# Drains behind GpSimd's masking selects and 32 more dummy passes ahead of the first transposes, in a windowed attention followed by a two-layer product

## The chip, the cores and the metric

The kernel runs on one core of a Trainium2 chip. The metric is the device time of one execution in microseconds (us): 211.31 us in the median of three runs, 210.72 to 211.42. The core has a matrix engine (TensorE, PE in the profile; its weight loads are listed apart as PEld), VectorE (DVE), ScalarE (ACT), GpSimd (POOL) and SyncE (SP), each with an instruction queue of its own that it works through in order, and 16 engines for transfers (DMA) that all queues share.

## The reference

Four batches of eight heads, 768 positions of width 64. A position sees the first four positions ("sinks") and the 128 positions up to itself. The result goes through two matrix products with a squared relu between them.

```python
scores = scale * np.matmul(q, k.transpose(0, 1, 3, 2))
is_sink = pos[None, :] < int(n_sink)                       # 4
in_window = (rel >= 0) & (rel < int(window))               # 128
scores = np.where(is_sink | in_window, scores, -1000000000.0)
a = np.exp(scores - np.max(scores, axis=-1, keepdims=True))
a = a / (np.sum(a, axis=-1, keepdims=True) + 1e-09)
out = np.matmul(a, v)
...
x = out.transpose(0, 2, 1, 3).reshape(B * S, H * D)        # 3072 x 512
r = np.maximum(x @ w_in, 0.0)                              # 512 x 2048
return (r * r) @ w_out                                     # 2048 x 512
```

## The kernel before

**An order written by hand.** The kernel first collects some 890 operations (`op(...)`), each with a function that issues its instructions, the engines it may run on, and what it must come after. Then `Plan.run` walks through the string `ORDER` and issues them one by one: `57p+26` is operation 57 on TensorE (p), with 26 dummy passes ahead of it; v, a, g and s stand for VectorE, ScalarE, GpSimd and SyncE. So the order in every queue is fixed, and an engine that waits for one operation holds all that stand behind it in its queue.

**Attention.** For each batch `b` the rows of q and k come in, are transposed (by TensorE for batches 0 and 1, by transposing transfers of SyncE for 2 and 3, line 392), and then worked on in three strips `s` of 256 positions. For a strip and a pair of heads `m`, TensorE makes scores of the window in a PSUM tile `ps` (line 554), ScalarE takes their exponential into `expm` (line 574), and the entries outside the window are set to zero in `expm` by a mask operation (`domask`, lines 579 to 591). TensorE then multiplies the masked tile with v into `po` (line 633), together with the sinks' part (line 608), and VectorE divides by the sum (lines 648, 649) into `xn_sb`. That is brought into the layout of the product's left operand (`px` at line 678, or a transposing transfer) for layer 1 (lines 708 and 874) and layer 2 (lines 969 and 1088).

**The mask operations.** For the strips after the first the order gives each mask to VectorE, as one product with a triangle of ones (line 586), or to GpSimd, as two selects by position (`affine_select` in `triangles`, line 198), each over half of the tile's columns, 128 x 512 elements. Sixteen of the mask operations are GpSimd's; the selects that build the constants at the start use the same function or one of their own, but are not called from `domask`.

**GpSimd's queue.** GpSimd issues in the same queue the loads of w_in (line 278), w_out (line 284), v (line 342) and of q and k (line 331), all of which convert from float32 to bfloat16 on the way. In the timeline of GpSimd such a load occupies it for 0.5 to 1.1 us while it is issued; the transfer itself runs on, and its landing is what the reader of the data waits for. Selects and loads thus stand in one line, for instance `26g 116g` ... `107g` ... `27g 28g`: the last load of w_in, two mask operations, then loads of k.

**The dummy passes.** `warm` (line 168) issues as many matmuls of the identity with itself into the tile that the operation behind it is about to overwrite as `ORDER` asks for with `+n`. Nobody reads what they write. The order asks for them three times: 26 ahead of operation 57, the first transposes, 12 ahead of 69 and 1 ahead of 70. They wait for the identity (line 224) alone; the transposes behind them wait for ScalarE's copy of the first loaded rows (line 179).

Of the kernel before, what the change touches and what calls it, by code (L numbers as in the profile page):

```python
# [15 lines left out]
ALU = mybir.AluOpType  # L16

ORDER = """
0v 8s 9s 1v 56a 55a 3g 7a 10s 57p+26 58p 60v 11s 5g 6g 19g 4g 20g 67v 69p+12 21g 68g 59a 12s 13s 70p+1 83p 71a 61v
72a 14s 15s 22g 23g 84p 63p 102p 65v 85a 62a 86a 24g 25g 79g 103p 106a 73v 74v 64p 75p 76p 104a 66v 91p 113p 78v 93a  # L20
87p 77a 115a 89p 88v 105v 80v 90v 95p 92p 94a 26g 116g 81p 107g 96v 114p 82a 97p 119p 27g 28g 29g 30g 31g 32g 33g
108p 98v 117a 99p 109p 100a 118v 120p 111p 122p 101v 157p 121v 112v 123v 110v 163p 124p 169p 164v 126v 16s 125v 166p
# [52 lines left out]
class Plan:  # L75
# [5 lines left out]
    def op(self, kind, engines, run, after=(), takes=(), reads=(), dma=None, follow=(), late=()):  # L81
        o = Op(kind, engines.split(), run, after, takes, reads, dma, follow, late)
        o.group, o.idx = self.group, len(self.ops)
        self.ops.append(o)
        return o
# [21 lines left out]
def kernel(  # L107
# [11 lines left out]
    nc = tc.nc  # L119
# [24 lines left out]
    ident = consts.tile([128, 128], BF16)  # L144
# [17 lines left out]
    P = Plan(sizes)  # L162
    op = P.op

    def tile_of(slot, name, shape, dtype):
        return pools[slot.pool][slot.buf].tile(shape, dtype, name=name, tag=slot.pool)

    def warm(dst, key=None, h=0):


        for _ in range(P.dummies):
            ins = nc.tensor.matmul(dst, lhsT=ident, rhs=ident, start=True, stop=True,
                                   is_transpose=dst.dtype == BF16)
            if key:
                touch(key, "pe", ins, h)
# [10 lines left out]
    def touch(t, e, ins, *banks, alone=False):  # L186

        before = touched.setdefault(t, [])
        for e_, ins_, banks_, alone_ in before:
            apart = (e == "pe") != (e_ == "pe") or e != e_ and alone and alone_  # L190
            if apart and not set(banks) & set(banks_):
                tc.declare_no_dep(ins.ins, ins_.ins, reason="other bank")
        before.append((e, ins, banks, alone))


    def triangles(e_tile, i, n, fill=0.0):

        nc.gpsimd.affine_select(  # L198
            out=e_tile, in_=e_tile, compare_op=ALU.is_ge, fill=fill, base=i - 1,
            pattern=[[0, n], [1 if i else -1, 128]], channel_multiplier=-1 if i else 1,  # L200
        )
# [163 lines left out]
    def attention(b):  # L365
# [13 lines left out]
        def stage(g):  # L379
            P.group = ("prep", b, g)  # L380
            t0, n = groups[g]
# [16 lines left out]
            for m in range(NP // w) if b not in NATURAL else ():  # L398
# [16 lines left out]
                for part in ((1,), (0,)) if not casted else ((1, 0),):  # L415
                    def transpose_rows(e, m=m, bs=bs):

                        pt = bank_t[b, m, g] = tile_of(bs, "pt", [128, 2, 1024], BF16)
                        warm(pt[:, 0, 0:128], ("pt", b, m, g))
                        for j in range(w):  # L420
                            for ti in (1, 0):
                                for t in range(n):
                                    for h in range(2):
                                        r, o = slice(64 * h, 64 * h + 64), 64 * ((j * 2 + ti) * n + t)
                                        touch(("pt", b, m, g), e, nc.tensor.matmul(  # L425
                                            pt[:, h, o:o + 64],
                                            lhsT=qn_t[b, ti][r, t0 // 128 + t, 128 * (w * m + j):128 * (w * m + j) + 128],
                                            rhs=ident[r, r], is_transpose=True,
                                            start=(j == 0 and ti == 1 and t == 0),
                                            stop=(j == w - 1 and ti == 0 and t == n - 1)), h)  # L430

                    def transpose(e, m=m, bs=bs, part=part, casted=casted):
                        if 1 in part:
                            bank_t[b, m, g] = tile_of(bs, "pt", [128, 2, 1024], BF16)
                        pt = bank_t[b, m, g]
                        warm(pt[:, 0, 0:128], ("pt", b, m, g))
                        qs = {} if casted else {ti: qs_t.pop((b, m, ti, g)) for ti in part}
                        for j in range(w):
                            for ti in part:
                                for t in range(n):  # L440

                                    o = 128 * n * ti if w == 2 else 0
                                    h = j if w == 2 else ti
                                    touch(("pt", b, m, g), e, nc.tensor.matmul(
                                        pt[:, h, o + 128 * t:o + 128 * t + 128],
                                        lhsT=qn_t[b, ti][:, t0 // 128 + t, 128 * (m + 2 * j):128 * (m + 2 * j) + 128]
                                        if casted else qs[ti][:, t, 2 * j:2 * j + 2, :], rhs=ident, is_transpose=True,
                                        start=(t == 0 and (w == 1 or ti == 1)),
                                        stop=(t == n - 1 and (w == 1 or ti == 0))), h)
# [61 lines left out]
            def sink_scores(e):  # L511
                ps = bank_t["sink", b, g] = tile_of(bk, "pk", [128, 512], FP32)
                warm(ps[:, 0:128])
                for m in range(NP):
                    nc.tensor.matmul(ps[32 * m:32 * m + 32, 0:last - lo], lhsT=kb[:, 128 * m:128 * m + 32],  # L515
                                     rhs=qkT_sb[:, m, 0, lo // 128:last // 128, :], start=True, stop=True)
# [12 lines left out]
            for s in range(t0 // 256, last // 256):  # L529
# [3 lines left out]
                for m0 in range(2):  # L533
# [37 lines left out]
                    for j, m in enumerate((m0, m0 + 2)):  # L571
                        def expo(e, s=s, m=m, o=o, sl=exs[j]):
                            x = ex_t[b, s, m] = tile_of(sl, "expm", [128, 2, 512], BF16)
                            nc.scalar.activation(out=x[:, :, o:512], in_=bank_t["s", b, s, m][:, :, o:512],  # L574
                                                 func=AF.Exp, scale=scale)
                        ex = op(f"exp {512 - o}", "act", expo, after=[sc[j % len(sc)]],
                                takes=[exs[j]], reads=[banks[j]])

                        def domask(e, s=s, m=m, o=o):
                            x = ex_t[b, s, m]  # L580
                            if s == 0:
                                mk = mask0.rearrange("p h a c -> p h (a c)").to_broadcast([128, 2, 384])
                                nc.vector.tensor_mul(x[:, :, 128:512], x[:, :, 128:512], mk)
                            elif e == "dve":
                                y = x.rearrange("p h (i c) -> p (h i) c", i=2)
                                nc.vector.tensor_mul(y, y, tri.rearrange("p (o a) c -> p o (a c)", o=1).to_broadcast(
                                    [128, 4, 256]))
                            else:
                                y = x.rearrange("p h (i g c) -> p g (h i) c", i=2, g=2)
                                for i in range(2):  # L590
                                    triangles(y[:, i], i, 4)
                        if biased:
                            masked.append(ex)
                            continue
                        masked.append(op(f"mask {512 - o}", "pool dve" if s else "dve",
                                         domask, after=[ex, c_tri if s else late["masks"]]))
# [722 lines left out]
```

## Time and profile before

| | |
|---|---|
| median of three runs | 211.31 us (210.72 to 211.42) |
| the profiled execution's own time | 210.84 us |
| its span, first to last instruction | 209.1 us |
| TensorE's granted clock, mean | 0.994 |
| busy: TensorE, VectorE, ScalarE, GpSimd | 198.0, 170.7, 126.6, 96.2 us |
| GpSimd's 32 selects on `expm` | 24.6 us |
| GpSimd's issuing of loads of v, q and k | 21.5 + 17.6 + 17.7 us |
| software-issued transfers | 69248 packets, 12.59 MB |

Times in all views are us from the span's start unless marked ns. In the timeline a row gives start, duration, engine, line, operation and tiles, how many instructions were merged, and in brackets the idle time of the engine ahead of it with what ended it. In a view by source line the three numbers are the least, median and greatest duration in ns, and a line below gives the time from a load's issue to its landing in us. An engine's name with a q (POOLq) marks what its sequencer does without the engine. The chain of waits is followed back from the last instruction: at each step to what released it, or to the instruction ahead of it on its engine.

### The profile page before, as it was taken

The numbers are of one execution on the slowest core, as the hardware profiler recorded it, in microseconds if no ns is written. First come the engines' busy times: TensorE is split into PE (matmuls) and PEld (weight loads), VectorE is DVE, ScalarE is ACT, GpSimd is POOL, SyncE is SP. The second block draws the span as 40 slices with busy tenths as digits, with TensorE's granted clock in tenths as the row PEclk, the third lists the DMA queues.
The fourth block names the chain that finished last, engine by engine and source line by source line (L and its number), as shares of the span: only waits on it lengthen the run. The fifth ranks groups of instructions, "written<-read, shape, count | busy, mean of one in ns | idle before, by whom it ended". The sixth has DMA issues, their size and how long they took to land.

```text
span 209.1 us, 5720 instructions
## 1 busy us (share of the span) xinstructions
PE 198.0 (95%) x2402; PEld 162.7 (78%) x2407; DVE 170.7 (82%) x311; ACT 126.6 (61%) x168; POOL 96.2 (46%) x133
## 2 busy tenths in 40 slices
PE   5788999999999999999999999999999999999990
PEld 5547997578457765578798899998789999998990
DVE  3388668888599792689999999999999889999671
ACT  4693034568987726897854936889962067594100
POOL 7879774498899976391670089200050000000000
PEclk9999999999999999999999999999999999999997
DMA  5999999999999999999935249960036111200214
GB/s 158 276 186 205 176 194 215 166 156 205 155 156 133 120 117 157 125 156 190 215 93 155 50 34 103 130 192 0 3 74 144 40 67 38 102 0 3 100 54 150
DMA packets 93882, 26.10 MB, mean 125 GB/s; under 512 B 86816, under 2 KB 91552, under 8 KB 93856
## 3 DMA queue, kind: packets, MB, share of 16 engines
q0 software_dynamic: 69248, 12.59, 81.2%
q1 hardware_dynamic: 24280, 12.94, 29.5%
q8 instruction: 19, 0.31, 0.7%
q10 hardware_dynamic: 328, 0.20, 0.3%
q14 instruction: 7, 0.06, 0.1%
HBM read 27.30 MB, written 6.29 MB: 161 GB/s over the span
## 4 chain that ended last, share of the span: by engine, by line
PE 88%; ACT 3%; DMA 2%; DVE 2%; issue 1%; SPq 1%; POOL 0%; ACTq 0%
PE py L1088 28%; PE pm L708 20%; PE pm L874 17%; PE py L969 7%; PE po L633 6%; PE ps L554 5%; DMA qr<-in_q_dram 2%; ACT expm L574 2%; PE po L608 1%; PE px L678 1%; PE pt L425 1%; SPq L316 1%; PE pk L515 1%; ACT r L719 0%; DVE xn_sb L649 0%
## 5 line engine op out<-in xcount | busy, mean ns | idle before, releaser
L574 ACT ACTIVATE expm<-ps 128x1024 bf16<-128x1024 f32 (+1 forms) x48 | 44.3, 953 | 6.0 <-PE ps L554 5.8
L708 PE MATMUL pm<-xT,w_in_sb 128*128 128x256 bf16 (+1 forms) x320 | 44.1, 294 | 0.4 <-ACT r L719 0.4
L198 POOL TENSOR_SCALAR_AFFINE_SELECT expm<-expm 128x512 bf16<-128x512 bf16 x32 | 24.6, 801 | 40.2 <-ACT expm L574 40.1
L708 PEld LDWEIGHTS <-w_in_sb 128*128 128x128 bf16 x320 | 34.5, 114 | 6.9 <-issue 0.6
L1088 PEld LDWEIGHTS <-gT_sb 128*128 128x128 bf16 x336 | 31.1, 98 | 3.7 <-issue 0.2
L1088 PEld LDWEIGHTS <-sg 128*128 128x128 bf16 x240 | 22.4, 98 | 3.3 <-issue 0.6
L719 ACT ACTIVATE r<-pm 128x1024 bf16<-128x1024 f32 x14 | 14.3, 1024 | 17.4 <-PE pm L708 17.3
L874 PE MATMUL pm<-xs,w_in_sb 128*128 128x128 bf16 (+1 forms) x256 | 23.9, 246 | 0.0
L342 POOL DMA_DIRECT2D v<-in_v_dram x24 | 21.5, 903 | 4.6 <-DMA qn<-in_q_dram 3.8
L874 PEld LDWEIGHTS <-w_in_sb 128*128 128x128 bf16 x256 | 22.0, 114 | 0.2
L331 POOL DMA_DIRECT2D qn<-in_q_dram x20 | 17.6, 885 | 9.1 <-DMA w_out_sb<-in_moe_w_out_dram 4.5
L896 ACT ACTIVATE gT_sb<-r 128x1024 bf16<-128x1024 bf16 x19 | 19.5, 1053 | 2.4 <-DVE r L948 2.3
L1088 PE MATMUL py<-wt,gT_sb 128*128 128x256 bf16 x160 | 20.8, 273 | 0.0
L1088 PE MATMUL py<-wt,sg 128*128 128x256 bf16 x160 | 20.6, 273 | 0.0
L1088 PE MATMUL py<-w_out_sb,gT_sb 128*128 128x256 bf16 x144 | 18.5, 273 | 0.0
L331 POOL DMA_DIRECT2D qn<-in_k_dram x20 | 17.7, 890 | 1.6 <-issue 1.2
L649 DVE TENSOR_TENSOR xn_sb<-po,rc 128x512 bf16<-128x512 f32 (+1 forms) x28 | 17.2, 615 | 1.0
L936 ACT ACTIVATE r<-pm 128x1024 bf16<-128x1024 f32 x11 | 11.1, 1023 | 10.2 <-DVE sg L1046 5.8
L721 DVE TENSOR_SCALAR r<-pm 128x1024 bf16<-128x1024 f32 x10 | 12.1, 1228 | 5.7 <-PE pm L708 5.7
L874 PEld LDWEIGHTS <-qkT 128*128 128x128 bf16 x192 | 16.1, 114 | 0.5 <-issue 0.4
L921 DVE TENSOR_TENSOR t<-t,pm 128x512 f32<-128x512 f32 x24 | 15.5, 679 | 1.1 <-ACT t L179 0.5
L948 DVE CUSTOM_DVE_ANT_1 r<-pm,t 128x1024 bf16<-128x1024 f32 x12 | 14.4, 1218 | 1.9 <-PE pm L874 1.4
(95 smaller groups left out, 320.5 us busy)
## 6 DMA issues: line engine op xcount, KB each, us to landing
out_dram<-osb SPq DMA_DIRECT2D x11, 512.0 KB, 4.0
v<-in_v_dram POOLq DMA_DIRECT2D x24, 128.0 KB, 8.2
qn<-in_k_dram POOLq DMA_DIRECT2D x20, 128.0 KB, 9.4
qn<-in_q_dram POOLq DMA_DIRECT2D x20, 128.0 KB, 8.3
w_in_sb<-in_moe_w_in_dram POOLq DMA_DIRECT2D x4, 512.0 KB, 10.7
w_out_sb<-in_moe_w_out_dram POOLq DMA_DIRECT2D x4, 512.0 KB, 10.5
qr<-in_k_dram SPq DMA_DIRECT2D x4, 256.0 KB, 5.1
qr<-in_q_dram SPq DMA_DIRECT2D x4, 256.0 KB, 5.9
```

The costliest lines, as they stand in the source:

```text
L198: nc.gpsimd.affine_select(out=e_tile, in_=e_tile, compare_op=ALU.is_ge, fill=fill, base=i - 1, pattern=[[0, n], [1 if i else -1, 128]], ch ...
L331: nc.gpsimd.dma_start(out=qn_t[b, ti][:, t, :].rearrange("p (h d) -> p h d", d=D), in_=(q, k)[ti][b, :, 128 * t:128 * t + 128, :].rearrang ...
L342: nc.gpsimd.dma_start(out=v_sb[b % 2][:, t, :, 0:D], in_=v[b, :, 128 * t:128 * t + 128, :].rearrange("h p d -> p h d"))
L574: nc.scalar.activation(out=x[:, :, o:512], in_=bank_t["s", b, s, m][:, :, o:512], func=AF.Exp, scale=scale)
L649: touch(("po", b, s, m0), e, nc.vector.tensor_tensor(out=xn_sb[:, 2 * s:2 * s + 2, :].rearrange("p i (j q h d) -> q p j i h d", j=2, q=2, ...
L708: nc.tensor.matmul(pm[:, i, :], lhsT=w_in_sb[:, fb // 4, kb, fb % 4:512:4], rhs=xT[:, c0 // 256:(c0 + cw) // 256, kb, :], start=(kb == 0), ...
L874: touch(tag, e, nc.tensor.matmul(y[:, bk, :, i, :], lhsT=weights(name, f0 + i, a), rhs=rhs[:, a, :], start=fresh and i == 0 and a == 0, st ...
L896: nc.scalar.activation(out=d, in_=x, func=AF.Square)
L921: touch(tag, e, nc.vector.tensor_tensor(out=T["t"], in0=T["t"], in1=bank(bk), op=ALU.subtract), bk)
L948: touch(tag, e, nc.vector._custom_dve(TENSOR_ADD_SAT, out=r, in0=both(), in1=t, s0=3.4028235e38, s1=0.0), 0, 1)
L969: touch((b, u), e, nc.tensor.matmul(pm[:, i, :], lhsT=gT_sb[:, t, fb, :], rhs=w_out_sb[:, fb, :], start=(fb == 0), stop=(fb == NFB - 1)), i)
L1088: ins = nc.tensor.matmul(y_, lhsT=x[:, i, :], rhs=r_, start=(first or tail and n == 2) and i == 0, stop=i == HB - 1, skip_group_check=not ...
```

## The change

Two edits. `domask` issues a drain of GpSimd behind each of the two selects of a mask operation on GpSimd, 32 in all; a drain is an instruction in GpSimd's queue at which the queue stops until what is ahead of it is over. And the order asks for 58 dummy passes ahead of operation 57 instead of 26, while `warm` makes only the first 18 of a call full passes (128 rows, 128 columns) and those behind them passes of 32 rows and 32 columns. The calls with 12 and 1 passes stay as they were.

```diff
-0v 8s 9s 1v 56a 55a 3g 7a 10s 57p+26 58p 60v 11s 5g 6g 19g 4g 20g 67v 69p+12 21g 68g 59a 12s 13s 70p+1 83p 71a 61v
+0v 8s 9s 1v 56a 55a 3g 7a 10s 57p+58 58p 60v 11s 5g 6g 19g 4g 20g 67v 69p+12 21g 68g 59a 12s 13s 70p+1 83p 71a 61v
...
-        for _ in range(P.dummies):
-            ins = nc.tensor.matmul(dst, lhsT=ident, rhs=ident, start=True, stop=True,
+        for i in range(P.dummies):
+            m, n = (128, 128) if i < 18 else (32, 32)
+            ins = nc.tensor.matmul(dst[0:m, 0:n], lhsT=ident[0:m, 0:m], rhs=ident[0:m, 0:n], start=True, stop=True,
                                    is_transpose=dst.dtype == BF16)
...
                                 y = x.rearrange("p h (i g c) -> p g (h i) c", i=2, g=2)
                                 for i in range(2):
                                     triangles(y[:, i], i, 4)
+                                    nc.gpsimd.drain()
```

## The prediction

> **What bounds the kernel now.** I read the page first: busy shares, the chain of waits, the costliest groups.
>
> ```profile
> span 209.1 us, 5720 instructions
> ...
> PE 198.0 (95%) x2402; PEld 162.7 (78%) x2407; DVE 170.7 (82%) x311; ACT 126.6 (61%) x168; POOL 96.2 (46%) x133
> ...
> PE 88%; ACT 3%; DMA 2%; DVE 2%; issue 1%; SPq 1%; POOL 0%; ACTq 0%
> ```
>
> TensorE sets the time. It runs a fixed order in its queue, so what holds one matmul holds all behind it, and there is almost nothing later to win it back. GpSimd (POOL) is off the chain today, at 46% busy. Its 16 mask operations, of two selects each at line 198 on expm, get 32 drains. GpSimd is also the engine that issues the loads of weights, q, k and v, in one queue with the selects. So the question is what a drain waits for.
>
> **The drain's price.** No row shows a drain between two selects. The nearest are GpSimd's own drains at start and end: a view by source line, the timeline of GpSimd, and the landing of its last load.
>
> ```profile
> L1300 POOLq DRAIN  x1: 193/193/193, 0.4 to 0.4; - x1
> ...
> 0.41 0.11 POOL L1300 MEMSET const-uint8-127<- 128x1 uint8 x1
> ...
> L1314 POOLq DRAIN  x3: 45/93/4215, 152.6 to 208.9; - x3
> ...
> 152.58 2.96 POOL L198 TENSOR_SCALAR_AFFINE_SELECT expm<-expm 128x512 bf16<-128x512 bf16 x4 [20.35 <-ACT expm L574]
> ...
> L342 POOL DMA_DIRECT2D v<-in_v_dram x1: 903/903/903, 127.9 to 127.9; - x1
> ...
> DMA to landing us min/median/max: 6.4/6.4/6.4
> ```
>
> The drain at the start, with no load issued yet, ended at 0.38 + 0.19 = 0.57, some 0.05 us behind the last memset (0.41 + 0.11). The first at the end starts at 152.6 and takes 4.215, to 156.8, though the last select was over at 152.58 + 2.96 = 155.54: 1.2 us more, with all of GpSimd's loads issued since the first drain, the last of them landed at 127.9 + 6.4 = 134.3. The two after that, with nothing in between, took 45 to 93 ns. A drain of GpSimd thus seems to settle something besides the selects, and the loads are what differs. The lower end is 0.05 to 0.1 us per drain; the upper is that it waits until every load issued ahead of it has landed. I take the upper end, because the long row stands apart from the short ones in just this respect; a wait on loads in flight is my inference and is not shown.
>
> In the Trainium skill, "PSUM — Partial Sum Buffer", section "Engine vs sequencer instructions", a drain waits until the engine is fully idle; read as the selects alone that is the lower end and some 212 us, read with the transfers the upper. The long row at the end fits the second reading better.
>
> **First place, 15 us.** GpSimd's and TensorE's timelines, these selects by tile, and landings: of two single loads (min, median and max are one there), and last of all 40 loads of line 331.
>
> ```profile
> 15.28 2.39 POOL L198 TENSOR_SCALAR_AFFINE_SELECT expm<-expm 128x512 bf16<-128x512 bf16 x4 [1.19 <-ACT expm L574]
> ...
> L198 POOL TENSOR_SCALAR_AFFINE_SELECT expm<-expm x4: 628/628/628, 15.3 to 17.0; 128x512 bf16<-128x512 bf16 x4
> ...
> 17.74 1.25 PE L633 MATMUL po<-v,expm 128*128 128x65 bf16 x32
> ...
> L278 POOL DMA_DIRECT2D w_in_sb<-in_moe_w_in_dram x1: 803/803/803, 13.3 to 13.3; - x1
> ...
> DMA to landing us min/median/max: 11.6/11.6/11.6
> ...
> L331 POOL DMA_DIRECT2D qn<-in_k_dram x1: 904/904/904, 17.6 to 17.6; - x1
> ...
> DMA to landing us min/median/max: 8.2/8.2/8.2
> ...
> DMA to landing us min/median/max: 3.5/8.3/14.5
> ```
>
> The last load ahead of the selects is issued at 13.3 and lands 11.6 later, at 24.9. The drain behind the first select holds GpSimd until about 25.0. The other three selects (0.63 each) with their short drains (0.1) end near 27.2; before, at 15.28 + 2.39 = 17.67. TensorE needs the last two for the third quarter of its 32 value matmuls, half-way through that row, near 18.3. It resumes near 27.2: **+8.9**. Queued behind on GpSimd are the next loads, issued at 27.2 instead of 17.6. The first landed at 17.6 + 8.2 = 25.8 behind a backlog; with an empty queue I give it the shortest, 3.5, so 30.7: 4.9 late. That is less than TensorE's 8.9, which covers it; a cover of 4 us is left.
>
> **Second place, 65 to 75 us.**
>
> ```profile
> 64.34 0.88 POOL L331 DMA_DIRECT2D qn<-in_q_dram  x1
> 65.22 1.70 POOL L198 TENSOR_SCALAR_AFFINE_SELECT expm<-expm 128x512 bf16<-128x512 bf16 x2
> 66.88 0.89 POOL L331 DMA_DIRECT2D qn<-in_q_dram  x1
> 67.78 1.35 POOL L198 TENSOR_SCALAR_AFFINE_SELECT expm<-expm 128x512 bf16<-128x512 bf16 x2
> 69.09 1.78 POOL L342 DMA_DIRECT2D v<-in_v_dram  x2
> 70.85 0.89 POOL L331 DMA_DIRECT2D qn<-in_k_dram  x1
> 71.73 2.87 POOL L198 TENSOR_SCALAR_AFFINE_SELECT expm<-expm 128x512 bf16<-128x512 bf16 x4
> ...
> L331 POOL DMA_DIRECT2D qn<-in_q_dram x1: 883/883/883, 64.3 to 64.3; - x1
> ...
> DMA to landing us min/median/max: 14.5/14.5/14.5
> ...
> 70.06 0.92 PE L633 MATMUL po<-v,expm 128*128 128x65 bf16 x16
> ...
> 74.17 1.36 PE L633 MATMUL po<-v,expm 128*128 128x65 bf16 x32
> ...
> 59.23 18.27 SPq L392 DMA_TRANSPOSE qkT<-qn  x9
> ...
> 65.00:76.00 11.00, 10.87 (x193) 8.67 (x192) 9.23 (x18) 6.25 (x10) 10.99 (x15) 1.00 1.97 136
> ```
>
> The stretch's row (busy us of PE, PEld, DVE, ACT, POOL) has GpSimd busy 10.99 of 11.00: here it has no idle time to give. The load of 64.34 landed at 78.8; 4.9 later it is 83.7. The first drain holds the second select until 83.8, over at 84.6. TensorE's values of 70.06 need it; with 8.9 they would come at 79.0, so **+5.6**, total 14.5. Then each batch of loads is followed by a drain that waits for it on an almost empty queue, 3.5 from issue. A load is issued at 84.7 and landed at 88.2; second select to 88.9; three loads, the last issued at 90.8 and landed near 94.3; three selects and drains more to 96.6. The values of 74.17 need the last pair, and would come at 88.7 with 14.5: **+7.9**, total 22.4.
>
> **Later places.** The remaining selects are off the path:
>
> ```profile
> 93.15 1.72 POOL L198 TENSOR_SCALAR_AFFINE_SELECT expm<-expm 128x512 bf16<-128x512 bf16 x2
> 101.17 7.52 POOL L198 TENSOR_SCALAR_AFFINE_SELECT expm<-expm 128x512 bf16<-128x512 bf16 x8 [6.30 <-ACT expm L574]
> ...
> 103.42 0.66 PE L633 MATMUL po<-v,expm 128*128 128x65 bf16 x16
> ...
> L342 POOL DMA_DIRECT2D v<-in_v_dram x1: 876/876/876, 89.8 to 89.8; - x1
> ...
> DMA to landing us min/median/max: 13.3/13.3/13.3
> ```
>
> The selects of 93.15 are used at 103.42, 8.5 us after their end (94.87); their drain waits for the load of 89.8, which landed at 103.1 and, issued by a GpSimd whose queue is pressed less than before, slips less than TensorE does. I take 0; without that cover up to 3. Most of those of 101.17 have no load in flight and pay 0.1 each. Two mask operations among loads follow between 120 and 132, each up to 3 late; in the written order the values that use them (658p) stand between the two mask operations of 152.58 (672g, 664g), behind 20.35 us in which GpSimd was idle. Worth 0.
>
> **The dummy passes.** Weight loads of the passes by time, one row of the chain of waits, and the last stretch's row. The code gives 18 passes of 128 x 128 and 40 of 32 x 32 where 26 of 128 x 128 stood; the 12 and the 1 further on stay.
>
> ```profile
> 1.49 2.69 PEld L172 LDWEIGHTS <-ident 128*128 128x128 bf16 x26 [1.49 <-POOL ident L224]
> 5.53 0.45 PEld L444 LDWEIGHTS <-qs 128*128 128x128 bf16 x8 [1.35 <-ACT qs L179]
> 5.94 0.71 PEld L172 LDWEIGHTS <-ident 128*128 128x128 bf16 x12
> ...
> 29.93 0.57 PE pt L425 x32
> ...
> 202.60:209.10 6.50, 1.76 (x24) 1.50 (x22) 2.02 (x5) 0.00 (x0) 0.00 (x0) 0.80 0.47 164
> ```
>
> A pass took 2.69 / 26 = 0.103 us early on and 0.71 / 12 = 0.059 later: the clock had come up between. Eighteen end near 3.4. A small pass costs between 0.018 (0.57 / 32 of the small transposes) and 0.103, a full one; so 40 end between 4.1 and 7.5, against 5.53 when the first transposes are released. By columns (a quarter) it is 0.026, end near 4.5. I take 0. Even the upper end of 2 us, or a clock that comes up later, is hidden in the wait until 24.9, which loads set that do not depend on TensorE; without that cover it would cost up to 2.
>
> **The clock.** The last row's clock is 0.80 in the mean: half speed for 2.6 of 6.5 us, from about 206.5, some 4 us after TensorE's last matmul at 202.6. The three new stalls are 5 to 8 us long, so each should drop the clock, and by the start (1.5 to 5.5) it takes up to 4 us of work to come back, at half speed, up to 2 us lost. Behind the first stall a short burst at 25.7 uses part of it: 1.1. Behind the second it is hidden in the third; behind the third 1.9: **+3.0**. The Trainium skill ("TensorE: Matmul & The Clock Gate", "What's actually happening") gives windows of about 3.4 us for both; by it this term is 2.6.
>
> **Sum** against the profiled execution's own time, 210.84 (span 209.1, 1.7 around it; 0.5 under the median 211.31): 8.9 + 5.6 + 7.9 + 3.0 = 25.4, so **236**. Lower bound: SyncE's transposes, issued from 59.23 on, share the transfer engines; if the first stall lets the backlog clear, the load of 64.34 lands in 3.5, at 72.7, the second place costs only 2.6 (its chain of waits then ends at 85.7 against 83.1), and the sum is 222 without the clock's 3.0. Upper bound: if fresh loads need 6 to 8 us rather than 3.5, as that of 127.9 did with 6.4, two waits grow by 3 to 4 each, the selects of 93.15 come onto the path with 3, and a fourth stall costs another 1.9 of clock, 248 to 250.
>
> **Rivals.** (1) A fixed price: each drain costs the long row's 1.25 and waits for no landing. For: that row itself. Against: the 1.25 came after 72 loads at once. First place 3 x 1.3 less 0.6 of slack, 3.2; in the second, seven drains ahead of the last select's end, 9.1, of which TensorE's own 3.2 is already counted, so 5.9; at 101 four on the path, 5; sum 14.1, **225**. (2) A drain waits for selects alone, at 0.1 plus the 0.04 by which neighbours overlap today ((4 x 0.628 - 2.39) / 3): hidden at 15 us, where 18.3 - 17.67 = 0.6 of slack stands against 3 x 0.15; at 71.73 GpSimd is full and seven drains cost 1.0 on TensorE's path: **212**. (3) On the other side, not slower: selects alone, and short gaps between them let VectorE's masks beside them go sooner. The place is 65 to 76, the price limited by TensorE's idle time there, 11.00 - 10.87 = 0.13, and in the first 19 us by the chain; it decides where a drain costs under 0.02 more than the overlap that it replaces: **210.7**. (4) The drains are dropped or moved on build, so that only the passes act: 210.8 with up to 0.3 either way; counted with the third.
>
> **Chances.** Forecast 0.80, fixed price 0.06, selects alone 0.08, not slower 0.06. Of the third quarter, selects alone, 0.06 is over the bound; not slower splits evenly. About 0.3% (0.6 us) is what a measurement of this kernel can tell from no change. So slower 0.92, same 0.05, faster 0.03. The range 222 to 250 holds most of the forecast and the fixed price, and leaves out the rest, some 2 in 10.
>
> **What would show it.** Right: the second select at about 15.3 moves to 25, GpSimd's next load to 27; a TensorE idle stretch of 7 us before its values near 18, two more of 5 to 8 between 79 and 97; the loads after each come with short landings. Wrong: selects that still follow each other in under 0.8 us, then (2) or (3); all drains alike near 1.2, then (1). If the first stall shows and the later ones do not, the landing times in the second place are mis-sized.

## The result, and the profile after

The changed kernel takes 239.03 us in the median of six runs (237.44 to 240.01), the kernel before 211.01 us (210.05 to 211.72, six runs): a ratio of 1.1311, with a 95% interval of 1.1271 to 1.1351. The execution that was profiled is the fastest of the six, 237.44 us with a span of 235.7. The numbers below are differences between the two profiled executions, 26.6 us, which is 1.4 less than the difference of the medians. Ratios and their intervals leave out slow executions, of which two stand among the runs below: 242.51 us with the drains alone, and 336.52 of the kernel before. In the changed kernel the select is line 199, the drain 593, the values 635, the loads of w_in, q and k, and v 279, 332 and 343.

The head of the page, with the chain of waits (shares of the span):

```profile
span 235.7 us, 5821 instructions
...
PE 207.2 (88%) x2439; PEld 167.9 (71%) x2439; DVE 169.7 (72%) x311; ACT 126.6 (54%) x168; POOL 95.1 (40%) x133
...
PE 74%; issue 13%; POOLq 3%; POOL 3%; ACT 2%; DVE 2%; DMA 1%; ACTq 0%; SPq 0%
```

GpSimd has not become busier (95.1 us against 96.2), yet the chain has 13% of "issue" where it had 1%: some 31 us in which an engine stood still and waited for nothing that the profile shows. GpSimd's timeline says which engine:

```profile
15.95 0.63 POOL L199 TENSOR_SCALAR_AFFINE_SELECT expm<-expm 128x512 bf16<-128x512 bf16 x1 [1.98 <-ACT expm L575]
24.85 2.20 POOL L199 TENSOR_SCALAR_AFFINE_SELECT expm<-expm 128x512 bf16<-128x512 bf16 x3 [8.26 <-issue]
27.61 1.78 POOL L332 DMA_DIRECT2D qn<-in_k_dram  x2 [0.56 <-issue]
...
73.45 0.63 POOL L199 TENSOR_SCALAR_AFFINE_SELECT expm<-expm 128x512 bf16<-128x512 bf16 x1 [0.20 <-ACT expm L575]
85.52 0.64 POOL L199 TENSOR_SCALAR_AFFINE_SELECT expm<-expm 128x512 bf16<-128x512 bf16 x1 [11.45 <-issue]
86.72 0.89 POOL L332 DMA_DIRECT2D qn<-in_q_dram  x1 [0.56 <-issue]
87.62 0.65 POOL L199 TENSOR_SCALAR_AFFINE_SELECT expm<-expm 128x512 bf16<-128x512 bf16 x1
91.35 0.64 POOL L199 TENSOR_SCALAR_AFFINE_SELECT expm<-expm 128x512 bf16<-128x512 bf16 x1 [3.08 <-issue]
...
98.83 2.20 POOL L199 TENSOR_SCALAR_AFFINE_SELECT expm<-expm 128x512 bf16<-128x512 bf16 x3 [2.92 <-issue]
```

Between a select and the next stand idle times of 8.26, 11.45, 3.08 and 2.92 us. By the view by source line they are the drains, and only some of them; a second answer has the drains at the program's end:

```profile
L593 POOLq DRAIN  x32: 425/722/12032, 15.9 to 183.2; - x32
...
L1316 POOLq DRAIN  x3: 39/41/88, 184.4 to 235.4; - x3
```

The 32 drains run from 0.43 to 12.03 us with a median of 0.72; a drain's time runs from about the start of the select ahead of it, so most of that is the select's 0.63. And the long row at the end, 4.2 us before, is gone.

What a drain waits for is read from the loads ahead of it. Line by line: the load, with the time of its issue last, and below it the least, median and greatest time to its landing.

```profile
L279 POOL DMA_DIRECT2D w_in_sb<-in_moe_w_in_dram x1: 811/811/811, 13.2 to 13.2; - x1
...
DMA to landing us min/median/max: 11.2/11.2/11.2
...
L332 POOL DMA_DIRECT2D qn<-in_q_dram x1: 883/883/883, 72.4 to 72.4; - x1
...
DMA to landing us min/median/max: 11.8/12.1/12.4
...
L332 POOL DMA_DIRECT2D qn<-in_q_dram x1: 893/893/893, 86.7 to 86.7; - x1
...
DMA to landing us min/median/max: 4.5/4.5/4.5
```

The load of 13.2 lands at 24.4, and the second select begins at 24.85. The last load ahead of the drain at 73.45 is that of 72.4; it lands 12.4 later, at 84.8, and the next select begins at 85.52. That of 86.7 lands at 91.2; the next select is at 91.35.

TensorE's side, first after, then the same work before (rows that the prediction shows are left out):

```profile
25.54 0.57 PE L635 MATMUL po<-v,expm 128*128 128x65 bf16 x7 [6.75 <-POOL expm L199]
...
27.92 6.03 PE L710 MATMUL pm<-xT,w_in_sb 128*128 128x256 bf16 x32
33.88 0.41 PE L680 MATMUL px<-ident,xn_sb 64*128 64x64 bf16 x16
...
79.31 0.66 PE L635 MATMUL po<-v,expm 128*128 128x65 bf16 x16
...
86.22 1.01 PE L635 MATMUL po<-v,expm 128*128 128x65 bf16 x15 [4.49 <-POOL expm L199]
...
100.31 0.24 PE L635 MATMUL po<-v,expm 128*128 128x65 bf16 x1 [7.85 <-POOL expm L199]
...
102.35 2.93 PE L710 MATMUL pm<-xT,w_in_sb 128*128 128x512 bf16 x8
105.21 0.50 PE L555 MATMUL ps<-qkT 64*128 64x256 bf16 x8
...
231.23 1.06 PE L1090 MATMUL ya<-w_out_sb,gT_sb 128*128 128x128 bf16 x16
```

```profile
18.82 3.66 PE L708 MATMUL pm<-xT,w_in_sb 128*128 128x256 bf16 x32
22.42 0.41 PE L678 MATMUL px<-ident,xn_sb 64*128 64x64 bf16 x16
...
67.84 0.66 PE L633 MATMUL po<-v,expm 128*128 128x65 bf16 x16
...
75.36 1.89 PE L708 MATMUL pm<-xT,w_in_sb 128*128 128x512 bf16 x8
77.18 0.50 PE L554 MATMUL ps<-qkT 64*128 64x256 bf16 x8
...
203.30 1.06 PE L1088 MATMUL ya<-w_out_sb,gT_sb 128*128 128x128 bf16 x16
```

Subtracting row from row gives how late TensorE is: 9.1 us behind the first wait (27.92 against 18.82), 11.5 once 32 matmuls have taken 6.03 instead of 3.66, the same 11.5 still at 79.31, 27.0 at 102.35, 28.0 at 105.21, and 27.9 at the last row. Nothing is won back over 126 us. The end itself is shorter: 235.7 - 232.29 = 3.4 from the last matmul to the end of the span, against 209.1 - 204.36 = 4.7. So 27.9 - 1.3 = 26.6.

The two steps without a wait, 2.4 and 1.0, are the clock. Stretches of the changed kernel (busy us of PE, PEld, DVE, ACT, POOL, then the granted clock):

```profile
19.50:32.50 13.00, 6.20 (x45) 4.60 (x46) 2.24 (x8) 0.00 (x0) 6.80 (x9) 0.50 0.73 81
...
97.70:104.40 6.70, 3.55 (x29) 2.11 (x30) 2.30 (x5) 0.38 (x1) 4.72 (x7) 0.50 0.41 40
```

### The profile page after: what moved, and what is told of

It is laid out like the page before. It is cut to its first block, busy times and chain, and to the rows that moved or that the text cites. A ratio compares the mean times of both kernels' runs of the same rounds, so it can differ in the third digit from the quotient of the medians.

```text
span 235.7 us, 5821 instructions
## 1 busy us (share of the span) xinstructions
PE 207.2 (88%) x2439; PEld 167.9 (71%) x2439; DVE 169.7 (72%) x311; ACT 126.6 (54%) x168; POOL 95.1 (40%) x133
## 3 DMA queue, kind: packets, MB, share of 16 engines
q1 hardware_dynamic: 24280, 12.94, 24.4%
## 4 chain that ended last, share of the span: by engine, by line
PE 74%; issue 13%; POOLq 3%; POOL 3%; ACT 2%; DVE 2%; DMA 1%; ACTq 0%; SPq 0%
PE py L1090 23%; PE pm L710 20%; PE pm L876 15%; PE py L971 5%; PE ps L555 4%; PE po L635 4%; POOLq L593 3%; POOL qn L332 1%; DMA qr<-in_q_dram 1%; PE pt L445 1%; ACT expm L575 1%; POOL v L343 1%; DVE qs L182 1%; PE po L610 1%; PE ps L548 0%
## 5 line engine op out<-in xcount | busy, mean ns | idle before, releaser
L199 POOL TENSOR_SCALAR_AFFINE_SELECT expm<-expm 128x512 bf16<-128x512 bf16 x32 | 23.2, 724 | 75.1 <-ACT expm L575 41.9
L710 PE MATMUL pm<-xT,w_in_sb 128*128 128x256 bf16 (+1 forms) x320 | 47.5, 309 | 0.4 <-ACT r L721 0.4
L710 PEld LDWEIGHTS <-w_in_sb 128*128 128x128 bf16 x320 | 35.6, 118 | 9.2 <-issue 2.3
L635 PE MATMUL po<-v,expm 128*128 128x65 bf16 x352 | 16.3, 202 | 20.4 <-POOL expm L199 20.4
L635 PEld LDWEIGHTS <-expm 128*128 128x128 bf16 x352 | 13.9, 103 | 23.0 <-POOL expm L199 21.2
L650 DVE RECIPROCAL rc<-po 128x8 f32<-128x8 f32 (+1 forms) x28 | 5.5, 196 | 27.6 <-PE po L635 27.5
L876 PEld LDWEIGHTS <-w_in_sb 128*128 128x128 bf16 x256 | 22.0, 114 | 0.2
L898 ACT ACTIVATE gT_sb<-r 128x1024 bf16<-128x1024 bf16 x19 | 19.5, 1054 | 2.4 <-DVE r L950 2.3
## 6 DMA issues: line engine op xcount, KB each, us to landing
w_in_sb<-in_moe_w_in_dram POOLq DMA_DIRECT2D x4, 512.0 KB, 10.6
```

The costliest lines, as they stand in the source:

```text
L199: nc.gpsimd.affine_select(out=e_tile, in_=e_tile, compare_op=ALU.is_ge, fill=fill, base=i - 1, pattern=[[0, n], [1 if i else -1, 128]], ch ...
L635: touch(("po", b, s, m0), e, nc.tensor.matmul(pv[:, i, h2, :], lhsT=lhsT, rhs=rhs, start=(n_ == 0 and not s), stop=(n_ == len(mms) - 1)), j)
L710: nc.tensor.matmul(pm[:, i, :], lhsT=w_in_sb[:, fb // 4, kb, fb % 4:512:4], rhs=xT[:, c0 // 256:(c0 + cw) // 256, kb, :], start=(kb == 0), ...
L876: touch(tag, e, nc.tensor.matmul(y[:, bk, :, i, :], lhsT=weights(name, f0 + i, a), rhs=rhs[:, a, :], start=fresh and i == 0 and a == 0, st ...
L898: nc.scalar.activation(out=d, in_=x, func=AF.Square)
```

## The experiments

The theory put to test: a GpSimd drain waits until every load issued ahead of it has landed, and costs some 0.2 us where none is in flight. Its rivals: a price per drain, wherever it stands; and that the passes carry part of the loss. Each ratio is to executions of the kernel before on the same chip at the same time; their median is 211.06, 211.26 or 211.37 us, so two runs are compared by what each loses against its own.

**Drains alone.** The order's `57p+58` is put back to `57p+26` and `warm` to its old form.

> The 32 drains with the 26 full passes of before. Theory (a drain of GpSimd waits until every load issued ahead of it has landed, and the passes are hidden in the first wait): 238 to 239.5 us, as with both edits; full clock again from 5.2 us, first mask select back at 15.3, its drain until 24 to 25. Rival (part of the loss is the passes', through the full clock that came only at 8.9 us with both edits): 0.7 us or more below 239.0.

Measured: 239.93 us (237.98 to 242.51, four runs; 239.37 without that of 242.51, inside the theory's range), a ratio of 1.1332 (1.1286 to 1.1378). The interval covers the whole change's 1.1311, so the loss is the drains', and no part of it shows as the passes'.

**Passes alone.**

```diff
                                     triangles(y[:, i], i, 4)
-                                    nc.gpsimd.drain()
```

> The 18 full and 40 small passes without any drain. Theory (the passes cost nothing where the first wait covers them; here that cover is gone): full clock only near 8.9 us, TensorE 0.6 to 0.8 us late at the first strip's end, 211.4 to 211.8 us, a ratio of 1.002 to 1.004. Rival (the lateness is won back in slack ahead of 18 us): 211.0 us, ratio 1.000. Second rival (the passes themselves hold TensorE up): over 212 us.

Measured: 210.32 us (209.71 to 211.12, eleven runs) against 211.06, a ratio of 0.9965 (0.9948 to 0.9981). None of the three expectations: the passes gain 0.7 us. The last three runs below take this up.

**Drains where hardly a load is in flight.**

```diff
-                                    nc.gpsimd.drain()
+                                    if (b, s) in ((2, 2), (3, 2)):
+                                        nc.gpsimd.drain()
```

> Only the 12 drains of the third strips of the last two batches (the masks of 101 and 152 us), with the passes of before. Theory (loads in flight set the price): the first of them waits for the load issued at 89.8, until about 103.5; the others, with nothing in flight, add 0.2 each; 211 to 213 us. Rival (a price per drain of 0.8 us or more, wherever it stands, from 27.9 us over 32 drains): 12 x 0.87 = 10 us less some slack, 216 to 221 us.

Measured: 211.56 us, a ratio of 1.0015 (0.9995 to 1.0034): twelve drains for at most 0.7 us. The price per drain falls. The drains by source line (select included), and the selects behind the first of them in GpSimd's timeline:

```profile
L593 POOLq DRAIN  x12: 712/933/1609, 101.8 to 156.4; - x12
...
103.25 2.63 POOL L198 TENSOR_SCALAR_AFFINE_SELECT expm<-expm 128x512 bf16<-128x512 bf16 x3 [0.82 <-issue]
```

Its lowest, 0.71, is 0.08 more than the 0.63 of a select alone. The greatest fall to the first drain after a batch of loads that had all landed: the load issued at 89.04 landed 12.7 later, at 101.74, just ahead of that drain, and the next select still began 0.82 us after the end of the last. The first drain near 153 us, some 20 us behind the last loads, held its next select for 0.65. A drain thus has a remainder to settle behind landed loads, somewhat under the 1.2 at the end of the kernel before; the theory as I had put it did not have that.

**The first place alone**, and **the same with one load moved.** The first has the drains under `if b == 0`, 4 of them; the second also changes the order:

```diff
-87p 77a 115a 89p 88v 105v 80v 90v 95p 92p 94a 26g 116g 81p 107g 96v 114p 82a 97p 119p 27g 28g 29g 30g 31g 32g 33g
+87p 77a 115a 89p 88v 105v 80v 90v 95p 92p 94a 116g 81p 107g 26g 96v 114p 82a 97p 119p 27g 28g 29g 30g 31g 32g 33g
```

> Only the 4 drains of batch 0 (the first place), with the passes of before. Theory (the first drain waits for the last load of w_in, TensorE waits 8.8 and loses 2.6 more at half clock): 211.0 + 11.4 = 222.4 us, between 221.5 and 223. Rival (a price per drain of 0.87): 211.0 + 4 x 0.87 = 214.5 us.

> As the run with the 4 drains of batch 0, but the load of w_in that stood directly ahead of the two mask operations is issued behind them. Theory (the first drain waits for the youngest load ahead of it, now the one issued at 10.6, which landed at 22.3): the first drain ends 2 us earlier, near 22.6, and the time is about 2 us below that run's, 219.5 to 221. Rival (the drain waits for something that one load more or less doesn't change, such as the whole backlog of the queues): the same time as that run within 0.5 us.

Measured: 220.96 us, a ratio of 1.0469 (1.0442 to 1.0495), and 218.87 us, a ratio of 1.0358 (1.0311 to 1.0404). GpSimd's timeline of the first, then of the second with the last load that is left ahead of the drain:

```profile
13.39 0.81 POOL L278 DMA_DIRECT2D w_in_sb<-in_moe_w_in_dram  x1
16.18 0.63 POOL L198 TENSOR_SCALAR_AFFINE_SELECT expm<-expm 128x512 bf16<-128x512 bf16 x1 [1.98 <-ACT expm L574]
25.17 2.19 POOL L198 TENSOR_SCALAR_AFFINE_SELECT expm<-expm 128x512 bf16<-128x512 bf16 x3 [8.37 <-issue]
```

```profile
16.22 0.64 POOL L198 TENSOR_SCALAR_AFFINE_SELECT expm<-expm 128x512 bf16<-128x512 bf16 x1 [2.73 <-ACT expm L574]
21.76 2.20 POOL L198 TENSOR_SCALAR_AFFINE_SELECT expm<-expm 128x512 bf16<-128x512 bf16 x3 [4.91 <-issue]
...
L278 POOL DMA_DIRECT2D w_in_sb<-in_moe_w_in_dram x1: 770/770/770, 10.7 to 10.7; - x1
...
DMA to landing us min/median/max: 10.6/10.6/10.6
```

With the load of 13.39 out of the way, the drain ends 3.4 us earlier, right behind the landing of the one issued at 10.7 (10.6 later, at 21.4). Moving one load moved the wait: it is that load which the drain waits for. The loss against the kernel before fell less, from 9.9 us to 7.6. In the profiled execution, at 220.20 us the slowest of its four, TensorE is 3.6 us ahead of the first run until 74 us and only 0.7 from 81 us on. In between, VectorE's three masks of line 586 took 4.70 us from 70.7 on, two of them 2.0 and 2.1 each, beside a GpSimd without a gap, where the same three took 2.44 in the first run. Why they took longer was not tried, and whether they did in the three quicker executions (218.04 to 219.03) isn't known. The first run lies 0.5 below its expected range because half clock lasted from 20.5 to 30.6 there, and not past 32.5 as with all drains: the 32 matmuls behind the wait lost 1.2 us (4.84 against 3.66), where 2.6 was expected. The row of that stretch:

```profile
20.50:30.60 10.10, 3.98 (x35) 2.96 (x36) 2.24 (x8) 0.00 (x0) 4.57 (x7) 0.50 0.53 73
```

**The second place alone**: `if b == 1`, 8 drains.

> Only the 8 drains of batch 1 (the second place), with the passes of before. Theory (landings set the waits: the load of 64.34 lands at 78.8 as before, the second select is over near 79.8; from there to the last pair 14.9 us as with all drains, so the values of 74.65 come at 94.7, 20 late, and 1.6 more at half clock): 232.7 us, 231 to 234.5. Rival (each place adds its own fixed loss, so the second adds what is left of the whole, 28 - 11.4): 227.6 us. Rival (a price per drain of 0.87): 218 us.

Measured: 231.21 us, a ratio of 1.0936 (1.0888 to 1.0983), just inside the theory's range. The places don't add: 9.9 and 20.0 make 29.9, more than the 28.0 of all drains. GpSimd's timeline, the landing of the first load shown, and all transfers from 78.4 to 78.7 us:

```profile
64.70 0.88 POOL L331 DMA_DIRECT2D qn<-in_q_dram  x1
65.58 0.89 POOL L198 TENSOR_SCALAR_AFFINE_SELECT expm<-expm 128x512 bf16<-128x512 bf16 x1
78.66 0.64 POOL L198 TENSOR_SCALAR_AFFINE_SELECT expm<-expm 128x512 bf16<-128x512 bf16 x1 [12.18 <-issue]
...
DMA to landing us min/median/max: 13.5/13.5/13.5
...
q1 hardware_dynamic: 326, 0.07, 133.5%
```

The load of 64.70 lands 13.5 later, at 78.2; the next select follows at 78.66. That moment is set by GpSimd's own load, and not by all transfers: when the drain let go, SyncE's transfers (queue q1) were moving, 326 packets in 0.3 us, and none of GpSimd's. TensorE, not held up at 15 us, reaches its values at 70.5 and waits 8.83 us for them, instead of 4.49 with all drains: the time that the first place costs shortens the wait in the second.

**One drain for a mask operation instead of two**: `if i == 1`, 16 drains.

> One drain behind each mask operation (behind its second select) instead of two, 16 in all, with the passes of before. Theory (what counts is whether a drain stands between a load and a select that TensorE waits for, not how many): the first place loses 0.8 less, the values of the second wait are free at once, the last pair of the second place comes about 2.5 earlier; 235 to 237 us. Rival (a price per drain): half of the loss, 225 us.

Measured: 236.69 us, a ratio of 1.1203 (1.1148 to 1.1257), inside the theory's range: half of the drains keep nine tenths of the loss (25.4 us of 28.0). TensorE's timeline:

```profile
79.67 0.66 PE L635 MATMUL po<-v,expm 128*128 128x65 bf16 x16
...
97.37 0.24 PE L635 MATMUL po<-v,expm 128*128 128x65 bf16 x1 [13.51 <-POOL expm L198]
```

The wait for the second select is gone, as expected, and the one for the last pair has grown to 13.5: a drain taken away between two selects only hands its wait to the next drain.

**Eighteen full passes alone**: before's `warm`, `57p+18`, no drains.

> No drains, and 18 full passes alone ahead of the first transposes (the 40 small ones left out). Theory (the 40 small passes count for nothing towards the clock): full clock near 8.9 us and a time within 0.2 us of the run with 18 full and 40 small passes. Rival (small passes do keep the clock's window alive in part): full clock later than with them, near 12 us, and 0.5 us or more above that run.

Measured: 211.41 us, a ratio of 1.0010 (0.9989 to 1.0031), about 1 us above the run with 18 and 40, so the theory's 0.2 is missed. It isn't for the rival's reason either: in the two traces full clock came at 9.7 us here and at 11.9 in that run. When it comes says little of the passes. The 12 full passes near 6 us took 0.71 in the kernel before; in the run with twelve drains, with the same 26 passes ahead of them, and in the changed kernel they took:

```profile
6.27 1.32 PEld L172 LDWEIGHTS <-ident 128*128 128x128 bf16 x12
```

```profile
6.29 1.32 PEld L173 LDWEIGHTS <-ident 128*128 128x128 bf16 x12
```

So full clock was there by 5.9 us in one execution and not yet at 7.6 in another, with nothing changed ahead of it; the changed kernel's late clock needs no cause in the change. The Trainium skill ("TensorE: Matmul & The Clock Gate", "What's actually happening") has windows that run freely, without regard to the kernel's start, and the runs agree, but two of them lie at least 1.7 us apart, where it gives 0.5 us either way.

**What the passes gain.** In the kernel before, the transfers of 203 to 206 us hold a fetch of instructions (queue, kind: packets, MB, share of the 16 engines), and one of SyncE's last stores (line 1193) is issued meanwhile:

```profile
q8 instruction: 1, 0.02, 3.4%
```

```profile
204.22 0.89 SPq L1193 DMA_DIRECT2D out_dram<-osb  x1
```

With 64 more TensorE instructions the last such fetch is over some 4 us ahead of the last matmul's end. Three runs tell the number of instructions from the kind of passes: 26 full and 32 small passes, 18 full and 8 small, 26 full and 16 small, all without drains. The first:

```diff
-57p+26
+57p+58
...
-        for _ in range(P.dummies):
+        for i in range(P.dummies):
+            m, n = (128, 128) if i < 26 else (32, 32)
```

> No drains; the 26 full passes of before and 32 small ones behind them, so 64 TensorE instructions more than before, as with the 18 and 40. Theory (the passes alone gained 0.7 us because TensorE's last 16 KB of instructions, fetched at 203.1 us in before and over only behind the issue of the last stores, are fetched some 2 us earlier): the same gain, 210.3 us, a ratio of 0.995 to 0.998, with 3.6 to 4 us from the last matmul to the end instead of 4.6 to 5. Rival (fewer full passes are what gained): ratio 1.000.

> No drains; 18 full and 8 small passes, as many instructions as before. Theory (the count of instructions places the last fetch): no gain, ratio 0.999 to 1.002, 4.6 to 5 us from the last matmul to the end. Rival (fewer full passes are what gained): ratio near 0.9965.

> No drains; 26 full and 16 small passes, 32 instructions more than before. Theory (the last fetch moves about half as far, to end near the issue of the last stores or just ahead): some of the gain, ratio 0.996 to 0.999. Rival (only the number of full passes acts): ratio 1.000.

| passes | TensorE instructions against before | ratio (95%) | last matmul to end, us |
|---|---|---|---|
| 26 full + 32 small | 64 more | 0.9953 (0.9936 to 0.9970) | 3.4 |
| 18 full + 40 small | 64 more | 0.9965 (0.9948 to 0.9981) | 3.4 |
| 26 full + 16 small | 32 more | 0.9968 (0.9949 to 0.9987) | 3.4 |
| 18 full + 8 small | none | 1.0009 (0.9986 to 1.0031) | 4.5 |
| 18 full | 16 fewer | 1.0010 (0.9989 to 1.0031) | 4.1 |

The number decides, not the kind. The times to the end came out 0.1 to 0.2 us below what was expected of them. SyncE's timeline with 26 full and 32 small passes, and then the transfers of its 199 to 201 us, where the fetch now stands:

```profile
204.98 0.34 SPq L1194 DMA_DIRECT2D out_dram<-osb  x1
```

```profile
q8 instruction: 1, 0.02, 3.9%
```

The store's issue takes 0.34 us instead of 0.89. With 18 full and 8 small passes the fetch is back over the stores, and the issue took 0.56. That it is the fetch which slows the end is inferred from its place in these runs, not shown by a run that moves the fetch alone. Nor is the store's issue all of it: with 18 full passes the fetch was over by 205.0 us, ahead of the last matmul's end at 205.2, and the same issue took 0.34, yet the end still took 4.1 instead of 3.4. The kernel with 26 full and 32 small passes, 210.20 us, is half a per cent faster than the kernel before, and so than both kernels of this case.

## Why the prediction was right

The forecast was 236.0, in a range of 222 to 250; the median is 239.0. By its steps:

- **The drain's price.** That a drain waits for the loads was an inference there. It is now shown by the moved load (3.4 us earlier by one load), by the landings (24.4 and 24.85, 84.8 and 85.52, 91.2 and 91.35), and by drains with nothing in flight (ratio 1.0015). What it waits for are GpSimd's own loads: with the second place alone, the drain let go at 78.6 us in the middle of SyncE's transfers. The drain's own price was set at 0.1; three selects with drains between take 2.20 us, (2.20 - 0.63) / 2 = 0.78 from one to the next, where (2.39 - 0.63) / 3 = 0.59 stood before, so 0.2. The remainder behind landed loads was not in the prediction.

- **First place**, +8.9: 9.1, and GpSimd's next load at 27.61 (27.2 was forecast). That the late loads would stay covered held too: TensorE is 11.5 late at 33.88 and no later at 79.31.
- **Second place**, +5.6 and +7.9, 13.5 in all: 27.0 - 11.5 = 15.5. The places and the order of the waits were right, the sizes not quite; the first wait is 4.49 us, under the 5 to 8 that were to show. The load ahead of it was put at 83.7 and landed at 84.8, and that is near by luck: it was issued 8.0 later than before (72.37 against 64.34), not 4.9, and took 12.4 to land instead of 14.5. Fresh loads were given 3.5 us and took 4.5 and 4.2, and a load behind a drain started 0.56 late, which the prediction left out.
- **Later places**, 0: TensorE is 28.0 late at 105.21 and 27.9 at the end, with 20 more drains in between.
- **Dummy passes**, 0: the drains alone give 1.133, so the passes add nothing. Without the drains' cover, where up to 2 us of loss was feared, they gain 0.7, by a way that no step of the prediction had: with them the end of the kernel is 1.3 us shorter in the traces, the changed kernel's too.
- **Clock**, +3.0: 2.4 behind the first wait and 1.0 behind the third, 3.4 together; what the second lost was hidden in the third wait, as forecast. The first was mis-sized at 1.1: TensorE ran at half clock until past 32.5, 5 us after it had resumed, and not for 2. The third was put at 1.9, too high. One reading behind this step was wrong: the last matmul of the kernel before ends at 204.36, not 202.6, so the clock fell some 2 us behind it, and not 4.

The sum of 25.4 stands against 26.6 in the profiled execution; most of the rest of the 3 us to the median is that this execution is the fastest of its six. That the sum is so near is partly luck: the steps come to 28.0, 2.6 over the forecast, and the shorter end, which nobody forecast, takes 1.3 back. The mechanism, the places and the order of the waits were not luck. The rival of 1.25 us per drain (225) falls with the twelve drains, that of the selects alone (212) with the landings, and the two that were not slower (210.7 and 210.8) with the result.

## What to carry to other kernels

Where GpSimd both computes and issues loads, a drain is a wait for all loads that it has issued ahead. Before a drain is put behind one of its instructions, look up these loads and when they land: the price is that landing, not the drain, and the loads queued behind it start late as well. Where such a stop can't be avoided, issue loads behind it rather than halve the number of stops: one load moved took 2.3 us off a loss of 9.9, half of the drains taken away 2.6 off 28.0.

## What the runs showed of the hardware that was not expected

- The same stall (6.75 and 6.79 us in TensorE's timeline) cost half clock for 13 us in the changed kernel (from before 19.5 to past 32.5) and for 10 us in the run with the first place alone (20.5 to 30.6). A forecast of the clock's loss needs that spread.
- 32 or 64 more dummy instructions of TensorE at the start shortened the kernel's end by 1.3 us in the traces, as far as can be inferred by moving the last fetch of instructions away from the last stores. The Trainium skill ("Runtime: NRT & Kernel Launch", "Instruction fetch mechanics") has blocks of 16 KB, or 256 instructions, and calls the cost of a boundary mostly hidden; the fetch of 0.02 MB agrees with the size, and the ratio of 0.9953, if the fetch is its cause, is a case in which the cost is not hidden.
- A drain behind loads that have all landed can still take 0.6 to 1.2 us, once (0.65 and 0.82 with twelve drains, 1.2 at the end of the kernel before); the drains that follow it without new loads do not.
